# Attention and two expert layers on one core: the head's instructions ordered from durations, and the packed rows multiplied for two batches at once

## The chip, the cores and the metric

The kernel runs on one core of one Trainium2 chip. The metric is the device time of one execution in microseconds (us). Three runs of the kernel before gave 1274.31, 1274.45 and 1276.68 us, median 1274.45.

## The reference

Three parts follow each other. `q`, `k`, `v` have shape (4 batches, 8 heads, 576 tokens, 64), `p` has (4, 8, 32, 64), all float32; `w_in` and `w_out` hold float64 values.

```
packed = softmax(p @ k.T / 8) @ v                     # per batch and head: 32 x 64
out    = softmax(q @ packed.T / 8) @ packed           # 576 x 64
x      = out as (4*576 = 2304 tokens, 8*64 = 512)
h = x @ w_in   (512 x 2048);  g = h * sigmoid(1.702 h);  x1 = g @ w_out  (2048 x 512)
result = sum over 4 experts e of  probs[:, e] * (relu(x1 @ w1[e]) @ w2[e])     # 512 -> 1024 -> 512
```

## The kernel before, in words

**Precision.** A product of the two layers is made of three TensorE passes over float32r halves: each operand is split into a rounded part and the rest (`split`: a ScalarE copy and a VectorE or GpSimd subtraction), and `PARTS` names the three pairs that are summed. A float64 weight arrives as two 32-bit words; `convert` turns such a piece (128 x 512) into two halves by six VectorE instructions, two GpSimd instructions and one ScalarE copy. There are 32 such pieces: for each of the four passes of the first layer four of `w_in` and four of `w_out`.

**Attention.** A unit is one batch and four of its eight heads, so there are eight units; units 2b and 2b+1 are batch b. `pack(u)` makes the packed rows of a unit: PE transposes of k, scores, exp on ScalarE, transposes of the weights, the product with v, one more transpose, and a split into `pw`. `unpack(u)` makes the second attention's weights: transposes of q, scores, VectorE transposes and reductions, exp, a GpSimd product, and a split into the tile `a`. It never multiplies by the packed rows.

**First layer.** Since x = weights @ packed, the kernel multiplies `packed @ w_in` first. `packed_w(a, b)` does it for pass a (512 of the 2048 columns) and batch b: per group of four heads six matmuls of 128 x 512 into one PSUM bank, where half of each stationary tile is zero because the two pairs of heads must land on different rows, and then one split into `PW`. `l1_first` multiplies `PW` with `a` (six matmuls of 128 x 288 per step, two gelus on ScalarE, one VectorE subtraction); `l2_first` multiplies the result by `w_out` (twelve matmuls per step) and adds into `ACC`. Pass a goes over eight token blocks j (two per batch) and four chunks c. `l2_first` runs one block behind `l1_first`.

**Second layer.** `l1_second` and `l2_second` go over eight passes of four chunks and five token blocks. A chunk's `w1` and `w2` come as one raw tile and are split into two tiles; the four chunks of the next pass are split during the last block of a pass.

**What sets the order.** In the head three generators, two `lane`s of four units each and `conversions` for the first eight weight pieces, are advanced in turn, one stretch up to a `yield` per round, and one stretch of the list `moe` of first-layer steps behind them as soon as `ready()` says so by counts of rounds (`DELAY`, `START`, `WDELAY`). That written order is kept on every engine. After it a scheduler orders the rest by priority and by free buffers; `todo` says by which step which number of pieces must be converted.

**Buffers.** Nearly all tiles come from one pool `big` of 35 slots; raw weights have a pool `rawp` of 3 slots. PSUM has 8 banks in one pool.

Of the kernel before, what the change touches and what calls it, by code (L numbers as in the profile page):

```python
# [20 lines left out]
LANES = ((0, 2, 4, 6), (1, 3, 5, 7))  # L21
DELAY = 7
START = 12
WDELAY = 4
FIRST = "k0 k1 q0 q1 F F F"
# [3 lines left out]
def packed_attention_moe_kernel(  # L29
# [36 lines left out]
    big = ctx.enter_context(tc.tile_pool(name="big", bufs=35))  # L66
# [3 lines left out]
    rawp = ctx.enter_context(tc.tile_pool(name="rawp", bufs=3))  # L70
# [34 lines left out]
    state = {"dma": 0, "cvt": 0}  # L105

    def fetch_w():
# [16 lines left out]
        raw = rawp.tile([128, 512, 2], U32, tag="raw", name="raw")  # L124
# [7 lines left out]
        raws[key] = raw  # L132

    def make_w():
        for _ in convert():
            pass

    def convert():
# [18 lines left out]
        f32 = man.bitcast(F32)  # L157

# [7 lines left out]
        yield  # L166
# [6 lines left out]
        yield  # L173
# [6 lines left out]
        yield  # L180
        nc.scalar.copy(out=w[:, 0, :], in_=f32)
        yield
        nc.gpsimd.tensor_sub(out=w[:, 1, :], in0=f32, in1=w[:, 0, :].bitcast(F32))
        W[key] = w
        yield
# [7 lines left out]
    def load_kv(u):  # L193
# [15 lines left out]
        nc.sync.dma_start(out=vv, in_=v[b, h0 + 2:h0 + 4].rearrange("h (p r) d -> p h r d", r=R))  # L209
        raws["v", u] = [sl[0][:, m:], sl[1][:, m:], sl[2][:, :R * D], sl[2][:, R * D:m]]  # L210

    def load_q(u):
# [8 lines left out]
        raws["q", u] = pair  # L221

    def transposed_scores(pair, dst, scores):

        before = None
        for s in range(2):
            for j in range(2):
                ps = psum("ps_t")
                for r in range(3):
                    nc.tensor.transpose(ps[:, r * SP:(r + 1) * SP], pair[j][3 * s + r], ident[:SP, :SP])  # L230
                if s == 1 and j == 1:
                    scores(0)
                yield
                nc.scalar.copy(out=dst[:, j, s * HS:(s + 1) * HS], in_=ps[:, :HS])
        yield
        scores(1)
        yield

    def score(lhs, rhs, s):
        ps = psum("ps_s")  # L240
        for j in range(2):
            nc.tensor.matmul(  # L242
                out=ps[64 * j:64 * j + 64, :HS],
# [27 lines left out]

    def pack(u):
# [7 lines left out]
        def scores(s):  # L280
            pss.append(score(pT[:, u, :], kT, s))

        yield from transposed_scores([[x[:, 128 * r:128 * r + 128] for r in range(R)] for x in kr], kT, scores)
        for s in range(2):
            nc.vector.reduce_max(out=st[:, s:s + 1], in_=pss[s][:, :HS], axis=AX.X)
# [3 lines left out]
        yield  # L289
        for s in range(2):  # L290
            nc.scalar.activation(
                out=E[:, s * HS:(s + 1) * HS], in_=pss[s][:, :HS], func=AF.Exp,
                bias=st[:, 2:3], scale=scale, accum_out=st[:, 4 + s:5 + s],
            )
        yield
# [5 lines left out]
        for s in range(2):  # L301
            ps = psum("ps_e")
# [3 lines left out]
            yield  # L306
            dst = et[:, 3 * s:3 * s + 3, :].rearrange("p r n -> p (r n)")
            nc.scalar.copy(out=dst, in_=ps[:SP, :384])
        yield
# [11 lines left out]
        yield  # L321
# [394 lines left out]
```

## Time and profile before

| | us |
|---|---|
| median of 3 runs | 1274.45 |
| profiled execution | 1275.09 |
| its span | 1273.3 |
| PE busy | 1216.7 (96%) |
| VectorE (DVE) busy | 521.4 (41%) |
| ScalarE (ACT) busy | 351.5 (28%) |
| GpSimd (POOL) busy | 119.8 (9%) |

The granted TensorE clock over the execution is 0.985. The page divides the span into 40 slices of 31.8 us; PE is busy for nine tenths or more in all slices from the eighth on, and the second layer takes everything from 480.5 us on. PE's busy time counts a matmul from its start to its modelled end, so a busy PE can still be short of its best rate; the distance between starts in the timeline tells the rate.

### The profile page before, as it was taken

To read this page: it belongs to the slowest core of one execution; us is meant where nothing else is said; L and a number is where in the kernel's file an instruction comes from. 1 tells how busy PE (TensorE), PEld (TensorE's weight loads), DVE (VectorE), ACT (ScalarE), POOL (GpSimd) and SP (SyncE) were. 2 spreads that over 40 slices of the span, in tenths; PEclk is the share of its full clock that TensorE was granted. 3 is DMA by queue.
4 is the path that set the end of the run, shared out by engine and by line. 5 is a ranking of instruction groups with operands and counts; after the bars stand their busy time and mean duration, and the time that the engine had idled before them with its cause. 6 is when DMAs were issued, how large, how long until landed. Compare 5 with 4: busy or idle time off the path is not lost.

```text
span 1273.3 us, 16542 instructions
## 1 busy us (share of the span) xinstructions
PE 1216.7 (96%) x6912; PEld 1048.3 (82%) x6912; DVE 521.4 (41%) x929; ACT 351.5 (28%) x808; POOL 119.8 (9%) x150
## 2 busy tenths in 40 slices
PE   5489988999999999999999999999999999999998
PEld 3267877999999998888888888888888888888887
DVE  3873499776654441122233233223223224224122
ACT  4365754333334452132111112112012112112100
POOL 2330134221201330000000000000000000000000
PEclk9799998999999999999999999999999999999999
DMA  9633213221110010010001001002002002000011
GB/s 225 176 85 94 62 50 100 67 67 34 49 35 1 2 35 32 1 50 17 1 17 50 1 16 51 1 1 66 1 1 66 1 1 67 1 1 17 33 66 50
DMA packets 73482, 53.79 MB, mean 42 GB/s; under 512 B 43456, under 2 KB 62912, under 8 KB 73408
## 3 DMA queue, kind: packets, MB, share of 16 engines
q1 hardware_dynamic: 73408, 52.74, 14.1%
q8 instruction: 54, 0.88, 0.3%
q14 instruction: 20, 0.16, 0.0%
HBM read 48.01 MB, written 4.72 MB: 41 GB/s over the span
## 4 chain that ended last, share of the span: by engine, by line
PE 88%; DVE 7%; ACT 2%; issue 1%; POOL 1%; SPq 1%; DMA 1%; ACTq 0%; POOLq 0%; DVEq 0%
PE ps_g L487 31%; PE ps_o L515 31%; PE ps_acc L452 13%; PE ps_h L413 7%; PE ps_w L398 2%; PE ps_s L242 2%; DVE man L170 1%; PE ps_t L230 1%; DVE ex L174 1%; DVE man L177 1%; DVE ex L159 1%; DVE man L167 1%; DMA kv<-in_k_dram 1%; PE ps_v L313 1%; DVE h L427 0%
## 5 line engine op out<-in xcount | busy, mean ns | idle before, releaser
L515 PE MATMUL ps_o<-w,h 128*128 128x512 f32 x1728 | 421.7, 392 | 0.0
L487 PE MATMUL ps_g<-y,w 128*128 128x512 f32 (+1 forms) x1920 | 420.0, 368 | 0.0
L487 PEld LDWEIGHTS ps_g<-y,w 128*128 128x128 f32 x1920 | 338.6, 188 | 63.3
L515 PEld LDWEIGHTS ps_o<-w,h 128*128 128x128 f32 x1728 | 322.4, 188 | 68.0
L499 DVE SCALAR_TENSOR_TENSOR h<-ps_g,h 128x512 fp32r<-128x512 f32 (+1 forms) x160 | 102.2, 639 | 535.7 <-ACT h L498 535.7
L498 ACT ACTIVATE h<-ps_g 128x512 fp32r<-128x512 f32 (+1 forms) x160 | 89.0, 556 | 607.2 <-PE ps_g L487 607.2
L452 PE MATMUL ps_acc<-h,wout 128*128 128x288 f32 x1536 | 234.0, 300 | 9.6 <-ACT acc L468 6.1
L452 PEld LDWEIGHTS ps_acc<-h,wout 128*128 128x128 f32 x1536 | 214.5, 191 | 15.2 <-ACT acc L468 6.3
L413 PE MATMUL ps_h<-a,pw 128*128 128x288 f32 x768 | 126.0, 298 | 2.8 <-ACT pw L88 2.5
L413 PEld LDWEIGHTS ps_h<-a,pw 128*128 128x128 f32 x768 | 110.4, 188 | 6.8 <-ACT pw L88 2.9
L427 DVE TENSOR_TENSOR h<-g,h 128x288 fp32r<-128x288 f32 x128 | 61.8, 484 | 80.7 <-ACT g L426 80.7
L536 DVE SCALAR_TENSOR_TENSOR o<-ps_o,pr,o 128x512 f32<-128x512 f32 x126 | 86.1, 743 | 2.1 <-PE ps_o L515 2.1
L425 ACT ACTIVATE h<-ps_h 128x288 fp32r<-128x288 f32 x128 | 52.7, 412 | 106.4 <-PE ps_h L413 106.2
L89 DVE TENSOR_TENSOR w<-raw,w 128x512 fp32r<-128x512 f32 x64 | 45.1, 708 | 33.8 <-ACT w L88 33.7
L426 ACT ACTIVATE g<-ps_h 128x288 f32<-128x288 f32 x128 | 52.1, 408 | 7.6 <-DVE h L427 7.6
L88 ACT CAST w<-raw 128x512 fp32r<-128x512 f32 x64 | 38.9, 617 | 44.1 <-PE ps_o L515 44.1
L470 DVE TENSOR_TENSOR acc<-ps_acc,acc 128x288 f32<-128x288 f32 x96 | 43.4, 453 | 16.7 <-PE ps_acc L452 16.6
L398 PE MATMUL ps_w<-win,ppw 128*128 128x512 f32 x192 | 48.3, 399 | 0.0
L398 PEld LDWEIGHTS ps_w<-win,ppw 128*128 128x128 f32 x192 | 35.8, 192 | 7.4 <-issue 0.4
L89 POOL TENSOR_TENSOR y<-acc,y 128x288 fp32r<-128x288 f32 (+6 forms) x48 | 28.5, 610 | 67.1 <-ACT y L88 64.4
L163 POOL TENSOR_SCALAR ex<-ex 128x512 uint32<-128x512 uint32 x32 | 25.3, 789 | 94.8 <-DVE ex L160 92.6
L89 DVE TENSOR_TENSOR pw<-ps_w,pw 128x512 fp32r<-128x512 f32 x32 | 21.6, 682 | 24.7 <-ACT pw L88 24.7
(75 smaller groups left out, 535.5 us busy)
## 6 DMA issues: line engine op xcount, KB each, us to landing
raw<-in_moe_w_dram SPq DMA_DIRECT2D x64, 256.0 KB, 3.1
raw<-in_moe_w_in_dram SPq DMA_DIRECT2D x16, 512.0 KB, 4.4
raw<-in_moe_w_out_dram SPq DMA_DIRECT2D x16, 512.0 KB, 3.7
kv<-in_k_dram SPq DMA_DIRECT2D x32, 144.0 KB, 3.7
q<-in_q_dram SPq DMA_DIRECT2D x32, 144.0 KB, 2.9
out_dram<-o SPq DMA_DIRECT2D x18, 256.0 KB, 2.0
kv<-in_v_dram SPq DMA_DIRECT2D x16, 144.0 KB, 3.4
kv<-in_v_dram SPq DMA_DIRECT2D x8, 288.0 KB, 4.1
```

The source lines that it names most:

```text
L89: eng.tensor_sub(out=lo, in0=src, in1=hi.bitcast(F32))
L398: nc.tensor.matmul(out=ps, lhsT=pw[:, j, wp, :], rhs=W["in", a, 2 * g + j][:, xp, :], start=(m == 0), stop=(m == 5),)
L413: nc.tensor.matmul(out=ps[:, :HS], lhsT=PW[a, b, g][:, wp, c * 128:(c + 1) * 128], rhs=A[b * UG + g][:, xp, s * HS:(s + 1) * HS], start=(m ...
L425: nc.scalar.activation(out=h[:, 0, :], in_=ps[:, :HS], func=AF.Gelu_apprx_sigmoid)
L426: nc.scalar.activation(out=g32, in_=ps[:, :HS], func=AF.Gelu_apprx_sigmoid)
L427: nc.vector.tensor_sub(out=h[:, 1, :], in0=g32, in1=h[:, 0, :].bitcast(F32))
L452: nc.tensor.matmul(out=ps[:, :HS], lhsT=W["out", a, c][:, wp, t * 128:(t + 1) * 128], rhs=hid[a, j, c // 2][:, 2 * (c % 2) + hq, :], start ...
L487: nc.tensor.matmul(out=ps[:, :n], lhsT=w[:, wp, kk * 128:(kk + 1) * 128], rhs=Y[j, kk][:, xp, :], start=(m == 0), stop=(m == 3 * KD - 1),)
L498: nc.scalar.activation(out=h[:, 0, :n], in_=ps[:, :n], func=AF.Relu)
L499: nc.vector.scalar_tensor_tensor(out=h[:, 1, :n], in0=ps[:, :n], scalar=0.0, in1=h[:, 0, :n].bitcast(F32), op0=ALU.max, op1=ALU.subtract,)
L515: nc.tensor.matmul(out=accs[j][t], lhsT=h[:, hq, t * 128:(t + 1) * 128], rhs=w[:, wp, :], start=(c == 0 and m == 0), stop=(c == CPP - 1 an ...
L536: nc.vector.scalar_tensor_tensor(out=acc, in0=ps[t], scalar=pr[:, tok, e:e + 1], in1=acc, op0=ALU.mult, op1=ALU.add,)
```

## The change

**The head** is now issued by a class `Order`. Each part is a generator that yields, ahead of each piece of its work, the engine that the piece goes to, a duration in us and the PSUM banks it needs. `Order.run` keeps the time until which each engine is taken and always issues next the piece that can start first; a part's next piece can start 0.25 us (`HOP`) after its last. PSUM banks are counted, and `when` holds the time at which loads, packed rows, weights and tiles are there. The evictions of matmuls (`l1_out`, `l2_out`, `packed_w_out`) are parts of their own, and so are three lanes and the list of first-layer steps. A lane now has the order `p0 p2 u0 u2 p4 p6 u4 u6` (and the odd ones): four units are packed before the first is unpacked. Four more weight pieces are converted in the head, as soon as six units are done (`MORE`, `UNITS_DONE`).

**Packed rows.** In an odd batch the two pairs of heads swap their rows (`place`). So the stationary tile of a group holds a pair of an even batch beside the other pair of the odd batch, with no zeros, and three matmuls per pair serve both batches. The result stands in two PSUM banks, of which each batch owns half the rows, so a split is made of copies and subtractions of 64 x 512.

**Buffers.** Raw weights come from `big` too, which has 37 slots; `rawp` is gone.

In the rows below `kv` is a unit's k and v, `q` its q, `raw` a weight piece as loaded. On the queue that issues loads (SP), at the start, before:

```order
L203 DMA kv_122<-in_k_dram 96x6x64 x2
L203 DMA kv_123<-in_k_dram 96x6x64 x2
L207 DMA kv_122<-in_v_dram 96x384
L207 DMA kv_123<-in_v_dram 96x384
L209 DMA kv_124<-in_v_dram 96x2x384
L219 DMA q_132<-in_q_dram 96x6x64 x2
L219 DMA q_135<-in_q_dram 96x6x64 x2
L219 DMA q_138<-in_q_dram 96x6x64 x2
L219 DMA q_141<-in_q_dram 96x6x64 x2
L131 DMA raw<-in_moe_w_in_dram 128x1024 x3
```

and now:

```order
L279 DMA kv_119<-in_k_dram 96x6x64 x2
L279 DMA kv_120<-in_k_dram 96x6x64 x2
L283 DMA kv_119<-in_v_dram 96x384
L283 DMA kv_120<-in_v_dram 96x384
L285 DMA kv_121<-in_v_dram 96x2x384
L206 DMA raw<-in_moe_w_in_dram 128x1024 x4
```

The eight loads of q that stood ahead of the first weight piece stand behind it. On VectorE, where the last unpacking ends (`a` is its last tile), `h` is the subtraction of an `l1_first` step and `ex`, `man` belong to a conversion; before:

```order
L379 TENSOR_TENSOR a_1917<-t_1748,a_1917 128x576
L159 TENSOR_SCALAR ex<-raw 128x512 x2
L160 TENSOR_SCALAR ex<-ex 128x512
L167 TENSOR_SCALAR man<-raw 128x512
L160 TENSOR_SCALAR ex<-ex 128x512
L170 SCALAR_TENSOR_TENSOR man<-raw,man 128x512
L174 SCALAR_TENSOR_TENSOR ex<-raw,ex 128x512
L167 TENSOR_SCALAR man<-raw 128x512
L177 SCALAR_TENSOR_TENSOR man<-man,ex 128x512
L170 SCALAR_TENSOR_TENSOR man<-raw,man 128x512
L174 SCALAR_TENSOR_TENSOR ex<-raw,ex 128x512
L159 TENSOR_SCALAR ex<-raw 128x512
```

and now:

```order
L543 TENSOR_TENSOR h<-g_1730,h 128x288
L235 TENSOR_SCALAR ex<-raw 128x512
L236 TENSOR_SCALAR ex<-ex 128x512
L243 TENSOR_SCALAR man<-raw 128x512
L246 SCALAR_TENSOR_TENSOR man<-raw,man 128x512
L250 SCALAR_TENSOR_TENSOR ex<-raw,ex 128x512
L253 SCALAR_TENSOR_TENSOR man<-man,ex 128x512
L543 TENSOR_TENSOR h<-g_1771,h 128x288
```

Before, several conversions stand in a row with no `h` between them; now one conversion stands between two `h`. On ScalarE, in the last block of a pass of the second layer, with `h` the relu of an `l1_second` step, before:

```order
L498 ACTIVATE h_7101<-ps_g_7088 128x512
L88 CAST w1_7144<-raw_6657 128x512
L498 ACTIVATE h_7125<-ps_g_7112 128x512
L88 CAST w2_7147<-raw_6657 128x512
L88 CAST w1_7181<-raw_7150 128x512
L498 ACTIVATE h_7166<-ps_g_7153 128x512
```

and now:

```order
L616 ACTIVATE h_7056<-ps_g_7043 128x512
L156 CAST w2_7102<-raw_6612 128x512
L616 ACTIVATE h_7080<-ps_g_7067 128x512
L156 CAST w1_7136<-raw_7105 128x512
L156 CAST w2_7139<-raw_7105 128x512
L616 ACTIVATE h_7121<-ps_g_7108 128x512
```

The two copies of one raw tile have come together, and the last 24 raw tiles of the program all have the same slot, where three slots took turns before.

The diff, cut to its core:

```diff
-LANES = ((0, 2, 4, 6), (1, 3, 5, 7))
-FIRST = "k0 k1 q0 q1 F F F"
+LANES = ("p0 p2 u0 u2 p4 p6 u4 u6", "p1 p3 u1 u3 p5 p7 u5 u7")
+FIRST = "k0 k1 F F F F k2 k3 q0 q1 F F F F"
+HOP = 0.25
+UNITS_DONE = 6
+MORE = 4
...
+    def run(self, while_):
...
+                engine, us, banks = ask
+                if banks > self.free:
+                    continue
+                start = max(at, self.at.get(engine, 0.0))
+                if best is None or (start, rank) < best[0]:
+                    best, start_ = ((start, rank), p), start
...
+            engine, us, banks = p[2]
+            self.free -= banks
+            self.at[engine] = start + us
+            p[1] = start + us + HOP
+            p[2] = self.send(p, p[1])
...
-    big = ctx.enter_context(tc.tile_pool(name="big", bufs=35))
+    big = ctx.enter_context(tc.tile_pool(name="big", bufs=37))
-    rawp = ctx.enter_context(tc.tile_pool(name="rawp", bufs=3))
...
-            raw = rawp.tile([128, 2, 512], F32, tag="raw", name="raw")
+            raw = slot([128, 2, 512], F32, "raw")
...
+        yield "DVE", 0.83, 0
         nc.vector.tensor_scalar(out=ex, in0=hi, scalar1=0x7FF00000, scalar2=None, op0=ALU.bitwise_and)
...
-        yield
+        yield "DVE", 1.2, 0
...
-        yield
+        yield "DVE", 1.36, 0
...
+    def place(b, j):
+        o = 64 * ((b + j) % 2)
+        return slice(o, o + 64)
...
-        nc.gpsimd.memset(pw.bitcast(F32), 0.0)
...
-    def packed_w(a, b):
+    def packed_w(a, bp):
         for g in range(UG):
-            pw = packed[b * UG + g]
-            ps = psum("ps_w")
-            m = 0
+            yield "PE", 1.45, 2
+            pw = ppws[bp][:, g]
+            pss = []
             for j in range(2):
-                for wp, xp in PARTS:
+                ps = psum("ps_w")
+                for m, (wp, xp) in enumerate(PARTS):
                     nc.tensor.matmul(
                         out=ps, lhsT=pw[:, j, wp, :], rhs=W["in", a, 2 * g + j][:, xp, :],
-                        start=(m == 0), stop=(m == 5),
+                        start=(m == 0), stop=(m == 2),
                     )
-            split(PW[a, b, g][:, 0, :], PW[a, b, g][:, 1, :], ps, nc.vector)
+                pss.append(ps)
+            for b in (2 * bp, 2 * bp + 1):
+                PW[a, b, g] = slot([128, 2, 512], F32R, f"pw{g}")
+            order.add(packed_w_out(a, bp, g, pss), 1, clock())
+
+    def packed_w_out(a, bp, g, pss):
+        for b in (2 * bp, 2 * bp + 1):
+            t = PW[a, b, g]
+            yield "ACT", 1.2, 0
+            for j in range(2):
+                nc.scalar.copy(out=t[place(b, j), 0, :], in_=pss[j][place(b, j), :])
+            t_ = yield "DVE", 1.4, 0
+            for j in range(2):
+                r = place(b, j)
+                nc.vector.tensor_sub(out=t[r, 1, :], in0=pss[j][r, :], in1=t[r, 0, :].bitcast(F32))
...
-            if c == 1 and j % 2 == 1:
-                na, nb = (a, j // 2 + 1) if j < NB1 - 1 else (a + 1, 0)
+            if c == 1 and j % 4 == 3:
+                na, nb = (a, j // 4 + 1) if j < NB1 - 1 else (a + 1, 0)
...
+    def conversions(n, more):
+        for i in range(n + more):
+            if i >= n:
+                yield lambda: 0.0 if len(finished) >= UNITS_DONE else None
...
+        lanes = [lane(x) for x in LANES] + [conversions(2 * CPP, MORE)]
+        for i, x in enumerate(lanes):
+            order.add(x, 2 + i)
+        order.add(moe_lane(), 9)
+        order.run(lambda: any(p[3] in lanes for p in order.parts))
```

## Rows read from the trace of the kernel before

**Rows 1.** Windows: us, busy (xcount) of PE, PEld, DVE, ACT, POOL; PEclk, DMA, GB/s.

```profile
13.00:62.30 49.30, 27.53 (x240) 17.16 (x240) 36.06 (x69) 20.12 (x58) 15.80 (x17) 0.79 0.77 204
62.30:161.70 99.40, 89.60 (x876) 74.14 (x873) 51.93 (x111) 64.57 (x171) 18.13 (x28) 0.97 0.31 81
161.70:240.00 78.30, 66.72 (x430) 62.24 (x431) 74.00 (x128) 35.20 (x82) 31.49 (x27) 0.93 0.28 85
240.00:480.50 240.50, 240.44 (x1715) 234.34 (x1715) 135.56 (x270) 96.06 (x261) 51.88 (x70) 1.00 0.11 33
480.50:1273.30 792.80, 788.84 (x3643) 657.38 (x3641) 221.13 (x342) 132.38 (x234) 0.90 (x2) 1.00 0.07 24
```

**Rows 2.** Timeline of PE: start, duration, line, tile, count, idle before.

```profile
53.39 1.82 PE L242 MATMUL ps_s<-kT,pT 128*64 128x288 f32 x4 [17.02 <-ACT kT L234]
...
62.30 0.38 PE L413 MATMUL ps_h<-a,pw 128*128 128x288 f32 x1
...
160.15 1.54 PE L242 MATMUL ps_s<-qT,pT 128*64 128x288 f32 x8
...
191.99 1.57 PE L452 MATMUL ps_acc<-h,wout 128*128 128x288 f32 x5 [6.09 <-ACT acc L468]
...
292.33 2.93 PE L398 MATMUL ps_w<-win,ppw 128*128 128x512 f32 x12
295.10 0.96 PE L413 MATMUL ps_h<-a,pw 128*128 128x288 f32 x6
295.90 1.76 PE L452 MATMUL ps_acc<-h,wout 128*128 128x288 f32 x12
297.50 0.96 PE L413 MATMUL ps_h<-a,pw 128*128 128x288 f32 x6
```

**Rows 3.** Groups by line, VectorE, up to 62.3 us: busy, mean ns, idle.

```profile
L170 DVE SCALAR_TENSOR_TENSOR man<-raw,man 128x512 f32<-128x512 uint32 x5 | 5.3, 1055 | 0.2
L174 DVE SCALAR_TENSOR_TENSOR ex<-raw,ex 128x512 uint32<-128x512 uint32 x5 | 3.5, 702 | 0.5 <-POOL ex L163 0.5
L177 DVE SCALAR_TENSOR_TENSOR man<-man,ex 128x512 f32<-128x512 f32 x5 | 3.5, 692 | 0.2
...
L167 DVE TENSOR_SCALAR man<-raw 128x512 uint32<-128x512 uint32 x5 | 3.2, 633 | 0.0
L159 DVE TENSOR_SCALAR ex<-raw 128x512 uint32<-128x512 uint32 x6 | 3.0, 497 | 0.0
L160 DVE TENSOR_SCALAR ex<-ex 128x512 uint32<-128x512 uint32 x6 | 2.6, 428 | 0.2
```

**Rows 4.** Groups by line and shape, up to 240 us: busy, mean ns.

```profile
L89 DVE TENSOR_TENSOR pw<-ps_w,pw 128x512 fp32r<-128x512 f32 x12 | 7.8, 667 | 1.9 <-ACT pw L88 1.9
L425 ACT ACT_TABLE_LOAD x6 | 7.7, 1283 | 0.1
L88 ACT CAST pw<-ps_w 128x512 fp32r<-128x512 f32 x12 | 7.0, 589 | 6.0 <-PE ps_w L398 6.0
L308 ACT COPY kv<-ps_e 96x384 f32<-96x384 f32 x16 | 6.8, 496 | 0.0
```

**Rows 5.** Timeline of ScalarE around one change of its function table.

```profile
92.59 1.28 ACT L425 ACT_TABLE_LOAD   x1
93.88 0.41 ACT L425 ACTIVATE h<-ps_h 128x288 fp32r<-128x288 f32 x1
```

**Rows 6.** Loads: one tile's issues (ns, first and last start); sizes and landing.

```profile
L219 SPq DMA_DIRECT2D q<-in_q_dram x32: 312/505/1426, 11.9 to 134.4; - x32
raw<-in_moe_w_in_dram SPq DMA_DIRECT2D x16, 512.0 KB, 4.4
raw<-in_moe_w_dram SPq DMA_DIRECT2D x64, 256.0 KB, 3.1
```

**Rows 7.** Timeline of ScalarE in a pass's last block, second layer.

```profile
665.77 0.60 ACT L498 ACTIVATE h<-ps_g 128x512 fp32r<-128x512 f32 x1 [2.10 <-PE ps_g L487]
671.24 0.60 ACT L498 ACTIVATE h<-ps_g 128x512 fp32r<-128x512 f32 x1 [2.10 <-PE ps_g L487]
```

More of the change, by code (lines that the diff above doesn't have):

```diff
@@ L105, in packed_attention_moe_kernel, with arrives @@
     state = {"dma": 0, "cvt": 0}
+    order = Order(8)
+    when = {}
+    DMA = {"at": 2.0}
+    def arrives(key, mbytes):
+        DMA["at"] = max(DMA["at"], order.at.get("now", 0.0)) + mbytes / 0.235
+        when[key] = DMA["at"] + 2.0
     def fetch_w():
@@ L123, in fetch_w @@
             return
-        raw = rawp.tile([128, 512, 2], U32, tag="raw", name="raw")
+        raw = slot([128, 512, 2], U32, "raw")
         flat = raw.rearrange("p f two -> p (f two)")
@@ L132, in fetch_w @@
         raws[key] = raw
+        arrives(("raw",) + key, 0.52)
     def make_w():
-        for _ in convert():
-            pass
+        order.drain(convert())
     def convert():
@@ L230, in transposed_scores, with score @@
                     nc.tensor.transpose(ps[:, r * SP:(r + 1) * SP], pair[j][3 * s + r], ident[:SP, :SP])
-                if s == 1 and j == 1:
-                    scores(0)
-                yield
+                t = yield "ACT", 0.4, 0
                 nc.scalar.copy(out=dst[:, j, s * HS:(s + 1) * HS], in_=ps[:, :HS])
[L235 to L239, printed above, removed]
+                order.free += 1
+        for s in range(2):
+            yield "PE", 0.6, 1
+            yield from scores(s)
+    def score(lhs, rhs, s, b=0):
         ps = psum("ps_s")
@@ L242, in score @@
             nc.tensor.matmul(
-                out=ps[64 * j:64 * j + 64, :HS],
+                out=ps[place(b, j), :HS],
                 lhsT=lhs[:, 64 * j:64 * j + 64],
@@ L423, in l1_first, with l1_out @@
         h = hid[a, j, c // 2][:, 2 * (c % 2):2 * (c % 2) + 2, :]
+        order.add(l1_out(h, ps), 1, clock())
+    def l1_out(h, ps):
+        yield "ACT", 0.82, 0
         g32 = gp.tile([128, HS], F32, tag="g", name="g32")
@@ L646, in packed_attention_moe_kernel, with lane @@
     loaded = set()
-    def lane(units_):
-        for i, u in enumerate(units_):
-            load(f"k{u} q{u}")
-            yield from pack(u)
-            if i + 1 < len(units_):
-                load(f"k{units_[i + 1]}")
-            yield from unpack(u)
-            done[u] = due["round"]
-    def conversions(n):
-        for _ in range(START):
-            yield
-        for _ in range(n):
+    finished = []
+    def lane(steps):
+        steps = steps.split()
+        for i, t in enumerate(steps):
+            u = int(t[1])
+            need = "kq"[t[0] == "u"] + t[1]
+            load(need)
+            yield lambda: when[need[0], u]
+            part = pack(u) if t[0] == "p" else unpack(u)
+            ask = next(part)
+            for n in range(1 << 30):
+                if n == 8 and i + 1 < len(steps):
+                    load("kq"[steps[i + 1][0] == "u"] + steps[i + 1][1])
+                t_ = yield ask
+                order.at["now"] = t_
+                try:
+                    ask = part.send(t_)
+                except StopIteration:
+                    break
+            if t[0] == "u":
+                finished.append(u)
+    def conversions(n, more):
+        for i in range(n + more):
+            if i >= n:
+                yield lambda: 0.0 if len(finished) >= UNITS_DONE else None
             while pieces[state["cvt"]] not in raws:
                 fetch_w()
-            if state["dma"] < min(n, state["cvt"] + 3):
+            if i >= n or state["dma"] < min(n, state["cvt"] + 3):
                 fetch_w()
+            key = pieces[state["cvt"]]
+            yield lambda: when[("raw",) + key]
             yield from convert()
-            done["w"] = due["round"]
     engines = {e.engine for e in (nc.tensor, nc.vector, nc.scalar, nc.gpsimd, nc.sync)}
@@ L676, in packed_attention_moe_kernel @@
         all_p()
-        lanes += [lane(LANES[0]), lane(LANES[1]), conversions(2 * CPP)]
         load(FIRST)
-        while lanes:
-            due["round"] += 1
-            lanes[:] = [x for x in lanes if next(x, 1) is None]
-            moe_step()
+        order.on = True
+        lanes = [lane(x) for x in LANES] + [conversions(2 * CPP, MORE)]
[3 more added lines that the diff above has]
+        order.run(lambda: any(p[3] in lanes for p in order.parts))
+        for p in list(order.parts):
+            order.finish(p)
     norm_probs()
```

193 lines of the change are left out of this document (123 added, 70 removed).

## The prediction, made before the changed kernel ran

> **What bounds the kernel now.** I read the windows by stage first, cut at events of PE's timeline: 62.3 us, where the first `l1_first` step starts; 161.7, where the last scores of the attention end; 480.5, where the second layer begins [rows 1, 2]. The reader is to see three kinds of stretch. From 240 us on PE is busy throughout, 240.4 of 240.5 us and then 788.8 of 792.8 [rows 1]: only fewer matmuls or a smaller distance between them help there. Up to 62.3 us PE is busy 27.5 of 49.3 us at a granted clock of 0.79, while VectorE has 36.1 us of work in the same stretch; PE stands 17.02 us ahead of the scores that start at 53.39, put down to a copy of ScalarE that stood behind other work in its queue [rows 1, 2]. Between 161.7 and 240 us VectorE is busy 74.0 of 78.3 us and PE loses time, once 6.09 us in one piece [rows 1, 2].
>
> The distances between starts give PE's rate where nothing waits: twelve `ps_w` matmuls from 292.33 to 295.10, 0.231 us each; six `ps_h` from 295.10 to 295.90 and twelve `ps_acc` from 295.90 to 297.50, 0.133 us each [rows 2]. With these I split the first layer at the last scores. Behind that point the order of before has 156 `ps_w`, 642 `ps_h` and 1338 `ps_acc` matmuls: 36.0 + 263.3 = 299.3 us. They took 480.5 - 161.7 = 318.8 us. So 19.5 us were lost there, and 240 to 480.5 shows no gap; the loss lies between 161.7 and 240.
>
> The same split gives the time after the change: end of the first layer = time of the last scores + matmuls left + time lost, and the second layer's 792.8 us behind it.
>
> **The sum, part by part.**
>
> *Matmuls.* Each pass and group needs six `ps_w` matmuls for two batches instead of twelve: 96 instead of 192 in all, 96 x 0.231 = 22.2 us less of PE work. Behind the last scores the new order has 72 `ps_w`, 654 `ps_h` and 1368 `ps_acc`: 16.6 + 268.9 = 285.5 us.
>
> *The splits of the packed product.* 32 copies and 32 subtractions of 128 x 512 become 64 and 64 of 64 x 512. No row shows half the partitions at this length. From below they cost half, so nothing is added; from above each costs as much as the full one, 0.589 and 0.667 us [rows 4]. A copy on 96 partitions of 384 columns took 0.496, near what its columns alone ask between 288 and 512, so I take the upper end: 18.8 us more on ScalarE, 21.3 on VectorE over the first layer. Eight and eight stand together behind each of six such places after the head, 4.7 us on ScalarE and 5.3 on VectorE, while about 4.8 us of PE steps lie between the product and its first reader. The odd batch is read only two blocks later, and so half of each eight is not urgent. I take nothing for that by itself; without that cover it is up to 1 us at each of the six places, and I keep 0 to 6 in the range. The GpSimd memsets that go away were in nobody's way.
>
> *Until the first `l1_first` step.* It now stands behind four packings, all eight conversions and two and a half unpackings. The last of its inputs comes from VectorE. Its work up to there is the 36.1 us of the old stretch [rows 1]; 2.5 conversions more (5.5 had run) at 1.055 + 0.702 + 0.692 + 0.633 + 0.497 + 0.428 = 4.0 us [rows 3], 10 us; eight 64 x 512 subtractions for one of 128 x 512, 4.7 us; the rest of two packings and the first transposes of a third unit, about 2 us. Together 53 us. It can start when the first weight piece lands: that load now takes the place of the first q, issued at 11.9 us, and a piece of `w_in` lands 4.4 us after its issue [rows 6], so 16.3 us. Without a single gap VectorE is through at 69. With as many gaps as the old stretch had (49.3 - 36.1 = 13.2 us) it is 82. I take 72, near the lower end, because work that needs no PE lies ready in its queue all the time; against the 62.3 of before that is 10 us later, with more done.
>
> *From there to the last scores.* The old stretch took 99.4 us, of which PE was busy 89.6 [rows 1]. Of PE's work 12 `ps_h`, 30 `ps_acc` and 12 `ps_w` leave it: 42 x 0.133 + 12 x 0.231 = 8.4 us. The layer's matmuls made 324 x 0.133 + 24 x 0.231 = 48.6 of the 89.6, so the attention had 41. Of its matmuls the new order leaves 105 of 120 transposes, 36 of 40 scores, 24 of 30 transposes of weights and 96 of 144 of the product with v behind the first `l1_first`: some five sixths, 7 us less. So 99.4 - 8.4 - 7 = 84 us if the old waits stay. Bounds: with PE dense it is 89.6 - 15.4 = 74, and if nothing is saved 99. VectorE has 10 us less to do there. ScalarE has more: functions are no longer done two units at a time, and the built order has 18 loads of its function table instead of 12, which the durations in the yields leave out. Six at 1.283 us [rows 4] are 7.7 us beside its 64.6 [rows 1]. I take 84, and the last scores end at 72 + 84 = 156.
>
> In the trace the next function starts 93.88 - 92.59 = 1.29 us after the load does [rows 5]. The Trainium skill, ScalarE: Activation LUTs, What ACT_TABLE_LOAD costs, puts a change of table at 1.283 us and another 1.38 of draining, 2.66 together; by it the six would cost 16 us of ScalarE and the whole would come out up to 8 us later, if ScalarE were the bound. The row shows no such second part.
>
> *After the last scores.* Before, at the end of the head the steps were due for four pieces more than had been converted; VectorE did conversions nine to twenty while PE had 15 `l1_first` steps and their partners, 36 us of PE for about 49 of VectorE. Subtractions for `ps_h` stood behind them. Now four pieces are converted in the head, and conversions nine to twenty lie beside 31 steps: 31 x 2.4 = 74 us of PE, and 12 x 4.0 + 31 x 0.45, with additions and eight to sixteen splits, about 70 of VectorE. That is below PE's time, but not by much. Bounds: nothing lost, and 10 us, half of the old loss. I take 4 us.
>
> *Second layer.* Its matmuls and their order are the same. I take 792.8 us again; the one raw slot is a rival, below.
>
> Sum: 156 + 285.5 + 4 = 445.5 for the end of the first layer against 480.5, 35 us less. The profiled execution took 1275.09 us for a span of 1273.3, so 1.8 us lie around it and 1240.1 follows; the median of the runs is 0.6 us lower than that execution, and I predict 1239.5.
>
> **The rivals.**
>
> *A: only the matmuls leave.* The head ends the later for all that was put in front of it, and the pile-up on VectorE is as large as ever: 1274.45 - 22.2 = 1252. For it: VectorE sets the pace in both stretches, and its work does not shrink but grows by the splits. Against it: conversions stand apart in the new order, one between two `h`.
>
> *B: the order does not do what it says.* The planner counts 0.83 + 1.2 + 1.36 = 3.39 us for a conversion's VectorE work where the rows say 4.0 [rows 3], and no table loads. Every engine keeps the written order, so one late piece holds all behind it. Then the first step comes at 82, the next stretch takes the old 99 us, and 10 us are lost behind it: 181 + 285.5 + 10 = 476.5, only 4 us less than before: 1270. For it: the 17.02 us wait of before came from just such a queue. Against: that order was not made from durations at all, and this one is wrong by a sixth.
>
> *C: slower, by the raw slot.* In the second layer a chunk's raw tile can be loaded only after the last split of the chunk before has read it, since the last 24 share a slot. One round is a landing of 3.1 us [rows 6], two copies of 0.6 and a last subtraction of 0.7 [rows 4], with the issue about 5.3 us; a chunk's step is 671.24 - 665.77 = 5.47 us [rows 7]. ScalarE stands at the copy in front of a relu until the load lands. If a landing takes 2 us more, each round is 1.8 us over the step; over 24 rounds that is 44 us, less the head's 35: 1283. It decides once a round is over 5.47 + 35/24 = 6.9 us. Against it: a chunk is split some 10 us before its first matmul, and a relu has a step's time to be late, so a small excess is absorbed.
>
> **Chances.** The forecast, as it stands, 0.62; A 0.18; B 0.13; C 0.07. The range: early at best with 69 + 74 = 143 for the last scores and nothing lost, which gives 1222.5; late, A and half of B, 1262. I put it at 1221 to 1262; the forecast's own is 1226 to 1248. About 0.2% (2.5 us) is what a measurement of this kernel tells from no change. B holds some of "the same" and, with worse luck in its queues, of "slower": faster 0.91, same 0.03, slower 0.06.
>
> **What would show each step right or wrong.** The first `ps_h` near 72 us, with VectorE busy nine tenths from about 17 us on; at 82 or later, B. The last scores at 150 to 162 us. Behind them PE without gaps of more than 1 us and 285 to 290 us to the second layer; gaps with VectorE named would be A. The second layer within 2 us of 792.8, with ScalarE's copies waiting for loads instead of for PE; a longer one is C. The prediction is wrong if the first layer ends after 468 us or before 428.

## The result

The kernel after takes 1263.74 us, the median of 4 runs (1261.61 to 1264.24), beside 1275.57 of the kernel before on the same chip: a ratio of 0.9904, 95% interval [0.9887, 0.9922]. It is faster by 11.8 us, just under one per cent. Forecast were 1239.5 us with a range from 1221 to 1262, so the direction was right and the size was not: the time lies 1.7 us above the range, and a third of the forecast gain is there.

| event, us of the span | before | forecast | after |
|---|---|---|---|
| first `ps_h` | 62.3 | 72 | 73.0 |
| last scores end | 161.7 | 156 | 174.5 |
| second layer begins | 479.0 | 445.5 | 467.2 |
| second layer lasts | 794.3 | 792.8 | 794.3 |
| span | 1273.3 | 1238.3 | 1261.5 |

The second layer's first `ps_g` of before starts at 479.0, not at the 480.5 where the windows of [rows 1] were cut; with that cut its length is the same in both, to a tenth.

### The profile page after: what moved, and what is told of

It is laid out like the page before. It is cut to its first block, busy times and chain, and to the rows that moved or that the text cites. A ratio compares the mean times of both kernels' runs of the same rounds, so it can differ in the third digit from the quotient of the medians.

```text
span 1261.5 us, 16419 instructions
## 1 busy us (share of the span) xinstructions
PE 1205.0 (96%) x6816; PEld 1038.0 (82%) x6816; DVE 538.9 (43%) x961; ACT 380.8 (30%) x846; POOL 116.4 (9%) x142
## 4 chain that ended last, share of the span: by engine, by line
PE 89%; DVE 4%; ACT 3%; issue 1%; DMA 1%; SPq 1%; POOL 1%; POOLq 0%; ACTq 0%; DVEq 0%
PE ps_g L607 31%; PE ps_o L632 31%; PE ps_acc L568 14%; PE ps_h L523 7%; PE ps_w L491 2%; PE ps_s L319 1%; PE ps_t L308 1%; SPq L279 1%; DMA raw<-in_moe_w_in_dram 1%; ACT L539 1%; DVE ex L250 0%; DVE man L246 0%; DVE pw L509 0%; ACT L374 0%; PE ps_v L399 0%
## 5 line engine op out<-in xcount | busy, mean ns | idle before, releaser
L568 PE MATMUL ps_acc<-h,wout 128*128 128x288 f32 x1536 | 230.3, 298 | 2.1 <-DVE h L543 2.0
L523 PE MATMUL ps_h<-a,pw 128*128 128x288 f32 x768 | 129.0, 303 | 16.6 <-ACT a L468 13.7
L523 PEld LDWEIGHTS ps_h<-a,pw 128*128 128x128 f32 x768 | 112.6, 193 | 20.1 <-ACT a L468 14.5
L543 DVE TENSOR_TENSOR h<-g,h 128x288 fp32r<-128x288 f32 x128 | 68.6, 537 | 72.0 <-ACT g L540 70.9
L509 DVE TENSOR_TENSOR pw<-ps_w,pw 64x512 fp32r<-64x512 f32 x64 | 43.0, 687 | 7.2 <-ACT pw L505 6.0
L239 POOL TENSOR_SCALAR ex<-ex 128x512 uint32<-128x512 uint32 x32 | 29.4, 920 | 125.1 <-DVE ex L236 121.4
L505 ACT CAST pw<-ps_w 64x512 fp32r<-64x512 f32 x64 | 36.4, 579 | 10.7 <-PE ps_w L491 8.4
L246 DVE SCALAR_TENSOR_TENSOR man<-raw,man 128x512 f32<-128x512 uint32 x32 | 27.8, 868 | 0.4
```

The lines of the kernel that those rows point to most:

```text
L523: nc.tensor.matmul(out=ps[:, :HS], lhsT=PW[a, b, g][:, wp, c * 128:(c + 1) * 128], rhs=A[b * UG + g][:, xp, s * HS:(s + 1) * HS], start=(m ...
L543: nc.vector.tensor_sub(out=h[:, 1, :], in0=g32, in1=h[:, 0, :].bitcast(F32))
L568: nc.tensor.matmul(out=ps[:, :HS], lhsT=W["out", a, c][:, wp, t * 128:(t + 1) * 128], rhs=hid[a, j, c // 2][:, 2 * (c % 2) + hq, :], start ...
```

## The profile after

The windows by stage, cut at the same events as [rows 1], and two pieces of the second stage below them. The columns are us, busy us (and count) of PE, PEld, DVE, ACT and POOL, the granted clock, the DMA share and GB/s.

```profile
13.00:73.00 60.00, 40.35 (x361) 25.50 (x357) 48.58 (x94) 28.42 (x78) 21.38 (x25) 0.71 0.79 215
73.00:174.50 101.50, 81.40 (x694) 66.19 (x692) 54.06 (x107) 70.20 (x160) 11.51 (x17) 0.85 0.26 67
174.50:240.00 65.50, 60.59 (x428) 58.84 (x427) 52.25 (x95) 33.41 (x83) 20.34 (x18) 0.97 0.13 41
240.00:467.20 227.20, 227.20 (x1672) 224.60 (x1670) 157.84 (x313) 109.77 (x284) 60.88 (x75) 1.00 0.14 43
467.20:1261.50 794.30, 790.34 (x3650) 658.67 (x3648) 223.41 (x344) 134.85 (x236) 1.61 (x2) 1.00 0.07 24
...
124.50:145.20 20.70, 15.62 (x160) 10.00 (x159) 8.23 (x18) 12.16 (x33) 2.36 (x5) 0.75 0.30 80
145.20:174.50 29.30, 19.11 (x134) 16.08 (x132) 21.34 (x37) 18.06 (x39) 4.30 (x4) 0.83 0.25 73
```

A stage's length less PE's busy time is what PE stood. Ahead of the first `ps_h` that is 19.7 us (before 21.8), from there to the last scores 20.1 (before 99.4 - 89.6 = 9.8), and behind them 4.9 (before 11.6). In the second stage no engine is full: VectorE has 54, ScalarE 70 and PE 81 of 101.5 us. From 13 us to the second layer PE is busy for 409.5 us, 13.3 less than before (422.8, without the last 1.5 us of [rows 1]'s fourth window); the 96 matmuls that left are 22.2 (the group `ps_w` is busy for 26.1 us where it was 48.3). The 8.9 between them are matmuls of the same kind that took longer, `ps_e` 347 ns on the mean where it was 279 and `ps_v` 263 where it was 221. They go with the granted clock, 0.85 in the second stage where it was 0.97, but no run changed the clock alone. So 22.2 less work, 8.9 given back by slower matmuls and 1.5 by idle time make the 11.8 us.

PE's timeline, as in [rows 2]: start, duration, line, tile, count, and in brackets the idle time and what ended it.

```profile
70.10 2.48 PE L319 MATMUL ps_s<-qT,pT 128*64 128x288 f32 x8 [8.36 <-DVE ex L235]
72.51 0.74 PE L308 MATMUL ps_t<-ident,q 96*128 96x96 f32 x3
72.96 0.59 PE L523 MATMUL ps_h<-a,pw 128*128 128x288 f32 x1
76.44 0.85 PE L523 MATMUL ps_h<-a,pw 128*128 128x288 f32 x2 [2.89 <-ACT a L468]
...
122.92 1.04 PE L568 MATMUL ps_acc<-h,wout 128*128 128x288 f32 x6
...
140.17 0.33 PE L422 MATMUL ps_pt<-ident,pp 128*128 128x128 f32 x1 [1.65 <-DVE pp L409]
...
143.26 2.15 PE L491 MATMUL ps_w<-win,ppw 128*128 128x512 f32 x6
145.25 0.96 PE L523 MATMUL ps_h<-a,pw 128*128 128x288 f32 x6
...
154.85 0.38 PE L523 MATMUL ps_h<-a,pw 128*128 128x288 f32 x1
165.09 1.57 PE L523 MATMUL ps_h<-a,pw 128*128 128x288 f32 x5 [9.86 <-ACT a L468]
...
173.82 0.71 PE L319 MATMUL ps_s<-qT,pT 128*64 128x288 f32 x4
...
215.83 0.43 PE L523 MATMUL ps_h<-a,pw 128*128 128x288 f32 x1 [2.82 <-ACT pw L505]
```

Two holes are new. Between the last `ps_acc` at 122.92 and the first `ps_w` behind it no step of the layer runs: the list stands at the product of batches 2 and 3, which needs the packed rows of units 4 to 7, and the last of them is transposed at 140.17. PE has only work of the attention in that time and is busy for 14.2 of 19.3 us. And at 154.85 a step of batch 2 starts; its first matmul reads unit 4's `a`, its second finds unit 5's missing, and the queue stands for 9.86 us with transposes and scores of the last unit behind it.

What happens in that hole stands in the timelines of ScalarE and of GpSimd, same columns:

```profile
156.73 1.28 ACT L457 ACT_TABLE_LOAD   x1 [3.01 <-DVE t L455]
158.03 1.26 ACT L457 ACTIVATE t<-t 128x576 f32<-128x576 f32 x2
162.73 0.67 ACT L468 CAST a<-t 128x576 fp32r<-128x576 f32 x1 [3.44 <-DVE t L465]
164.36 0.67 ACT L468 CAST a<-t 128x576 fp32r<-128x576 f32 x1 [0.97 <-DVE t L465]
164.94 0.39 ACT L310 COPY qT<-ps_t 128x288 f32<-128x288 f32 x1
165.35 1.28 ACT L539 ACT_TABLE_LOAD   x1
```

```profile
160.57 1.16 POOL L463 TENSOR_TENSOR t<-t,s 128x576 f32<-128x576 f32 x1 [17.35 <-DVE s L461]
162.36 1.16 POOL L463 TENSOR_TENSOR t<-t,s 128x576 f32<-128x576 f32 x1 [0.64 <-POOL t L463]
```

Both lanes unpack at once, units 5 and 6, since unit 4's `a` was finished at 146.1. They go side by side through the same chain: reductions on VectorE, a table load and two exponentials, sums, two GpSimd products, transposes, copies. ScalarE and GpSimd have two instructions at a time and then nothing until the others are through. VectorE, which has most of the chain, is busy for 8.40 of the 10.20 us from 154.9 to 165.1: here it comes near to being the bound, which the sums over the whole stage do not show. A lane is one unit after another, and there are two.

The splits of the packed product and VectorE's costliest conversion groups, which answer to [rows 3, 4]: group, count, busy us, mean ns, idle before.

```profile
L509 DVE TENSOR_TENSOR pw<-ps_w,pw 64x512 fp32r<-64x512 f32 x64 | 43.0, 687 | 7.2 <-ACT pw L505 6.0
L505 ACT CAST pw<-ps_w 64x512 fp32r<-64x512 f32 x64 | 36.4, 579 | 10.7 <-PE ps_w L491 8.4 <-DMA kv<-in_k_dram 0.3
...
L246 DVE SCALAR_TENSOR_TENSOR man<-raw,man 128x512 f32<-128x512 uint32 x32 | 27.8, 868 | 0.4
```

Half the partitions take the time of all: 0.579 and 0.687 us against 0.589 and 0.667 [rows 4]. The upper bound of that step holds. The six VectorE instructions of a conversion come to 3.7 us by their means over the kernel and to 4.1 up to the first `ps_h`, where the prediction had 4.0 and the planner counts 3.39.

The waits of ScalarE in the second layer, totals, times and longest in us; first of before (from 480 us), then of after:

```profile
ACT h L498 <- PE ps_g L487: 607.2, 160, 4.9
ACT w L88 <- PE ps_o L515: 44.1, 25, 2.1
```

```profile
ACT h L616 <- PE ps_g L607: 599.0, 157, 4.9
ACT w L156 <- DMA raw<-in_moe_w_dram: 24.6, 22, 1.9
ACT w L156 <- PE ps_o L632: 16.6, 15, 2.1
```

The copies wait for loads now, as the rival of the raw slot said, 22 times and at most 1.9 us, and the layer is no longer for it, 794.3 us in both kernels.

## The experiments

All at one sight. Each ratio is to runs of the kernel before on the same chip, whose median is 1275.57 us for after, 1276.42 for e1, e2, e4 and e5, 1276.20 for e3 and e8 to e10, and 1276.51 for e6 and e11 to e13; a difference of two medians from different sets is no better than about 1 us for that alone. "First" is the first `ps_h`, "last" the end of the last scores, in e1 to e13 to about 0.4 us; the next column is PE's busy time from 13 us to the second layer, the three behind it what PE stood (window less busy) to the first `ps_h`, to the last scores, and to the second layer. The last five columns are from one profiled execution each.

| kernel | median us | ratio to before | first / last | PE busy | idle 1 | idle 2 | idle 3 |
|---|---|---|---|---|---|---|---|
| before | 1275.57 | | 62.3 / 161.7 | 422.8 | 21.8 | 9.8 | 11.6 |
| after | 1263.74 | 0.9904 [0.9887, 0.9922] | 73.0 / 174.5 | 409.5 | 19.7 | 20.1 | 4.9 |
| e4 old product | 1274.59 | 0.9983 [0.9974, 0.9993] | 64.4 / 166.5 | 426.2 | 16.2 | 17.8 | 5.5 |
| e5 `MORE` 0 | 1275.74 | 0.9996 [0.9985, 1.0006] | 73.3 / 174.5 | 413.5 | 19.3 | 19.6 | 14.2 |
| e6 before, new product | 1273.51 | 0.9979 [0.9969, 0.9988] | 72.7 / 161.5 | 408.0 | 24.3 | 15.9 | 15.5 |
| e2 product later | 1257.13 | 0.9854 [0.9833, 0.9876] | 73.2 / 171.8 | 406.1 | 20.2 | 17.2 | 4.2 |
| e1 one table | 1252.58 | 0.9815 [0.9795, 0.9835] | 73.4 / 164.2 | 404.2 | 18.8 | 15.1 | 3.8 |
| e8 e1 and e2 | 1253.45 | 0.9812 [0.9790, 0.9834] | 73.2 / 166.8 | 408.9 | 17.8 | 15.0 | 3.9 |
| e9 before, one table | 1269.18 | 0.9940 [0.9925, 0.9955] | 62.6 / 156.9 | 422.2 | 21.1 | 5.8 | 12.3 |
| e10 e2, fewer loads | 1262.51 | 0.9890 [0.9875, 0.9904] | 70.6 / 171.8 | 406.9 | 19.3 | 19.3 | 7.6 |
| e3 four lanes | 1238.99 | 0.9716 [0.9688, 0.9744] | 61.5 / 132.5 | 401.2 | 10.1 | 9.6 | 5.6 |
| e11 four, old product | 1256.75 | 0.9848 [0.9833, 0.9862] | 59.2 / 135.2 | 431.7 | 6.5 | 8.8 | 1.1 |
| e12 e3 and e2 | 1240.71 | 0.9723 [0.9702, 0.9743] | 63.5 / 136.2 | 410.6 | 7.5 | 9.9 | 6.9 |
| e13 e3 and e1 | 1231.93 | 0.9652 [0.9637, 0.9667] | 62.3 / 126.3 | 399.7 | 11.9 | 4.3 | 4.5 |

### What each part is worth

**e4**, the kernel after with the product per batch, as before (stationary tiles half zero, one split of 128 x 512 per group); the core of it:

```diff
-            yield "PE", 1.45, 2
+            yield "PE", 1.45, 1
...
-            if c == 1 and j % 4 == 3:
-                na, nb = (a, j // 4 + 1) if j < NB1 - 1 else (a + 1, 0)
+            if c == 1 and j % 2 == 1:
+                na, nb = (a, j // 2 + 1) if j < NB1 - 1 else (a + 1, 0)
```

> The changed kernel with the product made for one batch at a time as before (192 matmuls, zeros in the stationary tiles, whole 128 x 512 splits), order and lanes of the change kept. If the matmuls are worth their 22.2 us and nothing else hangs on the product: 1286. Theory S: the product for batch 2 needs two packings instead of four and gives the steps earlier, so 6 to 12 us of the gap come back: 1274 to 1280, with the last scores before 170 us. Theory T: 1284 to 1288, since the loads stay.

The time is what theory S expected, at its lower end, with the last scores at 166.5. All of the change but the product gives 0.17%, about 2 us. It takes away half of the idle time behind the scores (11.6 to 5.5 us) and some ahead of the first step (21.8 to 16.2), and gives 8.0 back between them (9.8 to 17.8). The product gives the rest, 10.9 us by the medians and 10 by the ratios, half of its 22.2.

**e5**, no weight pieces beyond the eight in the head:

```diff
-MORE = 4
+MORE = 0
```

> The changed kernel without the four conversions more in the head (MORE = 0). Forecast's pile-up term: at the end of the head four pieces are due at once again, VectorE is behind for some 15 steps, and what is lost after the last scores grows from 7 us towards the 18 us of before: 1270 to 1275. Rival: the conversions were hoisted anyway and it stays at 1262 to 1266.

It comes out just above the 1275 expected. Its head ends where that of after does, and 12.0 us are lost behind it: the idle time there is 14.2 us instead of 4.9. PE's two longest waits there, and what ScalarE does ahead of the first:

```profile
213.28 2.93 PE L491 MATMUL ps_w<-win,ppw 128*128 128x512 f32 x6 [8.56 <-ACT acc L588]
227.49 0.61 PE L523 MATMUL ps_h<-a,pw 128*128 128x288 f32 x1 [4.98 <-ACT pw L505]
```

```profile
212.31 0.62 ACT L257 CAST wout<-man 128x512 fp32r<-128x512 f32 x1 [4.04 <-DVE man L253]
212.83 1.29 ACT L588 COPY acc<-ps_acc 128x288 f32<-128x288 f32 x4
```

The copies `acc`, which PE waits for, stand on ScalarE behind a copy that waits for a conversion on VectorE. The four early conversions are what removes this pile-up, as the prediction's step *After the last scores* had it.

**e6**, the kernel before with the new product alone; the line of the list, out of a longer edit:

```diff
-            if c == 1 and j % 2 == 1:
-                na, nb = (a, j // 2 + 1) if j < NB1 - 1 else (a + 1, 0)
+            if c == 1 and j % 4 == 3:
+                na, nb = (a, j // 4 + 1) if j < NB1 - 1 else (a + 1, 0)
```

> The kernel before with its own written order, with the two-batch product alone: 96 ps_w matmuls instead of 192, splits of 64x512, and the first step only behind four packings. Theory (what the product saves is mostly taken back by the wait for four packings, and the old order with its unit pairs 0 1 unpacked before 2 3 are packed makes that wait longest): the first ps_h moves from 62 to 80 or later, 1262 to 1276. Rival (only the matmuls leave, the wait is covered): 1252 to 1256.

The wait was shorter than expected (72.7, not 80), but the time is as the first theory said: 14.8 us less of PE work and 12.5 us more idle time, 4 of them with the pile-up behind the scores. It is 0.21% faster than before, 2 to 3 us. Neither part is worth much alone.

### What lengthens the stretch to the last scores

**e2**, the product of batches 2 and 3 two chunks later in the list:

```diff
-            if c == 1 and j % 4 == 3:
+            if c == (3 if (a, j) == (0, 3) else 1) and j % 4 == 3:
```

> The changed kernel with the product for batches 2 and 3 of the first pass put two chunks later in the list, behind the last steps of batch 1. Theory S: two l1 and three l2 steps, 6.4 us of PE, move from behind 145 us into the stretch 123 to 140 where PE had none, and the time falls by 4 to 7 us, to 1257 to 1260. Theory T: the units' chain is no faster and PE's later work is no less, 1262 to 1265.

It gives 6.6 us, as theory S expected. The place of the product blocks steps that were ready, but the hole at the unpacking is still there, 7.55 us up to 160.64 in its timeline.

**e1**, gelu computed as an exponential, which leaves the gelu out and needs one table load instead of 18:

```diff
-        nc.scalar.activation(out=h[:, 0, :], in_=ps[:, :HS], func=AF.Gelu_apprx_sigmoid)
-        nc.scalar.activation(out=g32, in_=ps[:, :HS], func=AF.Gelu_apprx_sigmoid)
+        nc.scalar.activation(out=h[:, 0, :], in_=ps[:, :HS], func=AF.Exp)
+        nc.scalar.activation(out=g32, in_=ps[:, :HS], func=AF.Exp)
```

> The changed kernel with the first layer's gelu computed as exp, so that ScalarE never changes its function table after the start (18 loads become 1 or 2); the result differs. Theory T, the added table loads stand in the chain of the units and made the stretch from the first step (73.0 us) to the last scores (174.5) 17 us longer than forecast: the last scores end at 160 us or earlier and the time falls by 12 to 20 us, to 1244 to 1252. Theory S, PE ran out of layer steps because the product for batches 2 and 3 waits for four packings and stands in the list ahead of steps that were ready: the gap without steps between 123 and 145 us stays, the last scores move by less than 6 us, 1258 to 1264.

**e9** is the same edit in the kernel before, without the gelu too, with one load instead of 12.

> The kernel before with gelu computed as exp, 12 table loads become 1 (the result differs). Theory T in its narrow form, the six added loads made the miss: before loses little by its own 11, under 5 us, 1271 to 1275. Theory T in its wide form, every load in the head stands in the chain at some 0.65 us: 11 loads give 7 us, 1268 to 1270, and of the 11.2 us that they cost after the change only 4 are new.

e1 lies between its two expectations: the last scores end at 164.2, and the time without a step of the layer shrinks from 19.3 us to 10.7 and does not vanish. The instructions of the two functions take the same time (0.414 and 0.413 us), so the edit removes the loads alone. e9 came out in its wide form. The loads cost 11.2 us after and, beside before on the same chip (1276.20), 7.0 before: 0.66 and 0.64 us each. So they cost alike in both kernels, about half their length, and the six new ones are worth some 4 us. They don't explain the 23 us that are missing.

**e8**, both edits in the kernel after, again without the gelu.

> The changed kernel with both edits: the product later in the list, and gelu computed as exp so that ScalarE loads its table once (the result differs). If table loads (11.2 us alone) and the place of the product (6.6 us alone) cost independent stretches, the sum of 17.8: 1246, with the last scores near 160 us. If they are two sides of the same gap, one takes most of the other: 1250 to 1252.

The two are not additive: 1253.45 is no better than e1 alone, and the idle time to the last scores is that of e1, 15.0 against 15.1 us. That fits two sides of one gap, the time in which no step is ready.

**e10**, e2 with a planner that counts a load against a piece when it chooses (but not in the time that it keeps), and so makes 10 of them instead of 18; without the lines that mark the pieces:

```diff
+LOAD = 1.3
...
-                if best is None or (start, rank) < best[0]:
-                    best, start_ = ((start, rank), p), start
+                load = LOAD if ask[3:] and ask[3] != self.fn else 0.0
+                if best is None or (start + load, rank) < best[0]:
+                    best, start_ = ((start + load, rank), p), start
```

> The changed kernel with the product later in the list, and with a planner that counts 1.3 us for a piece of ScalarE whose function (exp or gelu) is not the last one's: 10 table loads in the order instead of 18, the result unchanged. Theory T: eight of 17 loads gone give 8/17 of 11.2, 5 us: 1251 to 1254. If waiting for pieces of the same function costs as much as the loads saved: 1257 as without it.

It is 5.4 us slower than e2, outside both expectations. PE's `ps_h` waits 26.4 us for `a` in all, where it is 11.4 in e2. So a load avoided here is a piece put off. That with two lanes there was nothing to run in its place is the likely reason, and no run tried the same planner with four.

### More lanes

**e3**, the same units in four lanes of half the length:

```diff
-LANES = ("p0 p2 u0 u2 p4 p6 u4 u6", "p1 p3 u1 u3 p5 p7 u5 u7")
+LANES = ("p0 u0 p4 u4", "p1 u1 p5 u5", "p2 u2 p6 u6", "p3 u3 p7 u7")
```

> The changed kernel with four lanes of two units each, each packed and then unpacked (p0 u0 p4 u4 and so on) instead of two lanes. Theory L, the stretch to the last scores is long because each lane does its units one after the other, each waiting for PE, ScalarE and VectorE in turn, with no engine full (VectorE 54, ScalarE 70, PE 81 of 101 us): four chains side by side fill the gaps, last scores at 160 us or earlier, 1245 to 1258. Theory S: the first step and the product for batches 2 and 3 come no earlier, 1260 to 1268.

It takes 1238.99 us (1235.53 to 1243.27), 24.7 less than after and less than expected, and is the fastest kernel here that computes everything. The windows up to the second layer:

```profile
13.00:61.50 48.50, 38.36 (x378) 25.60 (x378) 38.17 (x80) 28.56 (x81) 17.13 (x21) 0.79 0.94 257
61.50:132.50 71.00, 61.41 (x571) 46.97 (x570) 54.01 (x112) 53.51 (x128) 17.86 (x21) 0.88 0.36 93
132.50:240.00 107.50, 101.91 (x734) 99.22 (x733) 79.60 (x152) 59.08 (x141) 24.51 (x23) 1.00 0.16 51
240.00:439.50 199.50, 199.50 (x1471) 197.44 (x1470) 134.48 (x266) 95.76 (x251) 54.82 (x70) 1.00 0.13 38
```

Against after, PE stands 25.3 us instead of 44.7 and is busy for 401.2 instead of 409.5, at the same count of matmuls: 19.4 + 8.3 are the 27.7 us by which the second layer begins sooner in these two executions (439.5 against 467.2). PE's groups from the first `ps_h` to the last scores, first of after (73.0 to 174.5), then of e3 (61.5 to 132.5), show which wait went:

```profile
L568 PE MATMUL ps_acc<-h,wout 128*128 128x288 f32 x169 | 28.5, 310 | 0.0
L523 PE MATMUL ps_h<-a,pw 128*128 128x288 f32 x114 | 23.8, 349 | 13.8 <-ACT a L468 13.7
...
L390 PE MATMUL ps_e<-ident,kT 128*96 128x128 f32 x24 | 4.6, 305 | 1.9 <-ACT kT L374 1.9
```

```profile
L568 PE MATMUL ps_acc<-h,wout 128*128 128x288 f32 x108 | 17.7, 307 | 0.0
L523 PE MATMUL ps_h<-a,pw 128*128 128x288 f32 x80 | 15.1, 327 | 0.0
...
L390 PE MATMUL ps_e<-ident,kT 128*96 128x128 f32 x24 | 5.6, 370 | 6.7 <-ACT kT L374 6.7
```

The 13.7 us for `a` are gone; the largest that is left is the exponential of a packing, 6.7. The stretch is 30.5 us shorter, but about half of that is work that moved behind it: 34 `ps_h`, 61 `ps_acc` and 12 `ps_w` fewer lie in it, 15.4 us at the prediction's rates. The list of steps stands here too, from 72.0 to 99.34, until the last of four pieces of `w_out` is converted (at 97.95). So it is not a list without a stop that makes e3 fast. Nor is it the loads: it makes 14 of them instead of 18, some 2.6 us at e1's price.

**e11**, four lanes with e4's product.

> The kernel with four lanes (e3, 1239 us) with the product per batch as before (192 ps_w matmuls with zeros, one 128x512 split per group). With two lanes the two-batch product was worth only 10.9 us (1274.6 against 1263.7) of the 22.2 us of matmuls it saves. Theory: the rest was lost because two lanes had nothing to run while the steps waited for four packings; with four lanes those packings come together, so the product is worth nearly all of its 22: 1257 to 1262 here, last scores within 4 us of e3's 132. Rival: the 64 extra copies and subtractions of 64x512 take it back on ScalarE and VectorE whatever the lanes do: 1248 to 1252 here.

The product is worth 1256.75 - 1238.99 = 17.8 us here, against 10.9 with two lanes; by the ratios it is 17 against 10, with intervals that leave about 5 us either way on the difference. e11 came out just under what the first theory said and well over the other's 1252. Part of what two lanes took from the product is given back by four, not all: PE stands 9 us longer with it than without, 25.3 against 16.4.

**e12**, four lanes and e2's place in the list.

> Four lanes (e3, 1239 us), with the product of batches 2 and 3 in pass 0 two chunks later in the list of steps. With two lanes this was worth 6.6 us. Theory (steps stood behind packings that two lanes brought late): with four lanes these packings are there in time, 1237 to 1241. Rival (the place in the list costs by itself, because its four split pairs fall on one spot): 1231 to 1234.

There is no gain, as the theory said: the ratios of e12 and e3 lie within each other's intervals. With four lanes the packings of batches 2 and 3 are there when the list comes to them: in e3 the last is transposed at 121.38, and the product starts at 134.66.

**e13**, four lanes and e1's single table, without the gelu.

> Four lanes (e3, 1239 us), with gelu computed as an exponential, so that ScalarE loads its function table once; the gelu is left out. With two lanes this was worth 11.2 us for 17 loads, some 0.65 us each. Theory (a load costs only because the one lane that waits for ScalarE has no other to run beside it): 1234 to 1239, at most 5 us. Rival (the loads delay ScalarE and so the head by themselves): again some 10 us, 1227 to 1230.

It gives 7.1 us for 13 loads, 0.54 each, between the two expectations. The two ratios leave 4 to 12 us, so whether four lanes hide any part of a load is not decided.

## Why the prediction was wrong

It was 23.2 us short in the span (1238.3 against 1261.5): 1.0 at the first `ps_h`, 17.5 from there to the last scores, 3.2 behind them, and 1.5 in the second layer, which is the misplaced cut. The first layer ended at 467.2, just inside the sign of 468 that the prediction set; its sign for the last scores, 150 to 162, was missed.

- *Until the first `l1_first` step*, 72: it started at 73.0, which is in part luck. VectorE's work was 48.6 us and not 53, and from 17 us on it was busy for 48.1 of 56.0, a little under the nine tenths expected. Only the first of the step's six matmuls had its inputs at 73.0; the second stood for 2.89 us, until 76.44, for unit 1's `a`.
- *From there to the last scores*, 84: **this step failed**, at 101.5 us, over the upper bound of 99 too. The count of the layer's matmuls was sound (114 `ps_h` as forecast, 169 `ps_acc` for 168), but "if the old waits stay" was not. PE's busy time was forecast at 89.6 - 15.4 = 74 and came to 81.4; its idle time at 10 and came to 20.1. In the old order a product needed two packings; the new one has a list that stops where four are needed (e2, 6.6 us), and two lanes that reach the unpackings together, 13.7 us of waiting for `a`. With four lanes of the same units that wait is gone and the whole takes 1239.0 us (e3). The step counted each engine's work and never the length of a lane's own chain. That the chains set the time is what e3 shows; how the 10.1 us of added idle time divide between the list and the lanes is open, since e1 and e2 overlap (e8).
- The slower pace of PE in that stretch is put down to the clock: the same 694 to 695 instructions took 81.4 us at a clock of 0.85 in after and 75.7 at 0.92 in e1. That rests on single executions, and no run changed the clock alone.
- *Function tables*: 7.7 us of ScalarE for six loads were counted and nothing was added for them. Measured, a load costs 0.54 to 0.66 us of the whole (e1, e9, e13), so six are some 4 us of the 17.5. The Trainium skill, ScalarE: Activation LUTs, What ACT_TABLE_LOAD costs, counts 2.66 us for a change; here the next function starts 158.03 - 156.73 = 1.30 us behind the start of the load, and the load at 165.35 starts 0.02 us behind the end of the copy ahead of it, so no second part shows after the change either.
- *Matmuls*: 22.2 us fewer were right as work, 48.3 to 26.1 for the group `ps_w`, and e11 against e3 gets 17.8 of them. With two lanes half is taken back (e4): the first `ps_h` comes at 73.0 instead of 64.4, since the first product waits for four packings.
- *After the last scores*, 285.5 + 4: it took 292.7, so 7.2 were lost, within the bounds of 0 to 10, and PE stood for 4.9. That the early conversions remove the pile-up was right (e5).
- *Splits*: half the partitions cost the same; the 2.82 us at 215.83 are such a place.
- *Rivals*: A gave 1252 and named VectorE behind the scores, and neither is so. B, "the order does not do what it says", came nearest with 1270, and its old 99 us for the stretch was almost the measured one; its first step at 82 was not. The planner's durations were short as it said, 3.39 us against 4.1 for a conversion in the head, but no run gave the planner the measured ones, so what they cost is open; e10, which counted loads in the choice, was slower. C is refuted: a round got waits for loads, and the layer's time stayed.

## What to carry to other kernels

Where no engine was full, the time of this head went by chains of dependent pieces and by how many of them were open at once (24.7 us from two to four lanes); count the chains as well as the work. An operation that serves two inputs at once also waits for both, so its saving is only worth as much as other work can fill that wait: 10.9 us with two lanes, 17.8 with four, 2 to 3 in the old order. A planner needs enough to choose from: with two lanes, one that avoided eight loads lost 5.4 us. Whether better durations would have helped was not tried.

## What the runs showed of the hardware

A wait of PE was followed by a slower clock. Windows of after: the hole at 154.9, the stretch behind it, and the next; columns as above.

```profile
154.90:165.10 10.20, 0.34 (x5) 0.12 (x2) 8.40 (x15) 3.95 (x6) 2.31 (x2) 0.65 0.22 68
165.10:170.40 5.30, 5.30 (x31) 5.28 (x32) 3.62 (x7) 3.22 (x7) 0.72 (x1) 0.70 0.00 0
170.40:174.50 4.10, 4.10 (x30) 2.90 (x28) 1.79 (x4) 2.59 (x7) 1.27 (x1) 1.00 0.44 132
```

PE works without a pause from 165.1 us on, yet the granted clock is 0.70 up to 170.4, so much of that stretch is at the lower level of 1.2 GHz, and it is 1.00 (2.4 GHz) only behind it. The timeline has both paces for the same work:

```profile
166.84 2.48 PE L568 MATMUL ps_acc<-h,wout 128*128 128x288 f32 x12
...
170.43 1.84 PE L568 MATMUL ps_acc<-h,wout 128*128 128x288 f32 x12
```

So a hole costs its length and something behind it. The Trainium skill, TensorE: Matmul & The Clock Gate, HAM oscillation — how this bites in real kernels, says that a wait of PE can bring its clock down again; this trace agrees (0.70 behind 9.86 us of waiting).
